# A convolution and a low-rank mixing block on one core: remainders of u read from PSUM, the first batch's last z added later in the chain, and a new order of the work

## The chip, the cores and the metric

The kernel runs on one core of a Trainium2 chip. The metric is the device time of one execution in microseconds (us). Five instruction queues matter: TensorE (PE, matmuls; its weight loads are shown apart as PEld), VectorE (DVE), ScalarE (ACT), GpSimd (POOL) and SyncE (SP), which here only issues DMAs. Each works through its own queue strictly in the order in which the program was written; an instruction that waits holds everything behind it on its engine. The on-chip memories are SBUF and PSUM; PSUM has eight banks of 2 KB per partition, and matmuls write only there.

## The reference

Eight batches of a sequence of 4224 positions and 192 features go through two stages. All arithmetic is float32; U, V and the two channel weights come in as float64.

```python
# stage 1: a causal convolution over 7 taps with softmax weights for each position and head
w = softmax(weight_gen, axis=-1)            # (8, 4224, 8 heads, 7 taps)
x_unf = x_pad[:, idx, :].reshape(B, S, K, H, group)      # group = 24 features a head
y = einsum('bshk,bskhg->bshg', w, x_unf).reshape(B, S, D)

# stage 2: mixing along the sequence (rank 32), then a channel MLP
u  = y + ((y^T @ U) @ V)^T                  # U: 4224 x 32, V: 32 x 4224
out = u + relu(u @ w_ch1) @ w_ch2           # 192 -> 768 -> 192
```

The mixing needs y of a whole batch (as z = U^T y) before u of any position of that batch is known.

## The kernel before

**Tiles and stages.** A batch is cut into 11 chunks of 3 x 128 positions, so there are 88 chunks (convolution) and 88 blocks (MLP), numbered through. Chunk or block i belongs to batch i // 11. The convolution runs about 11 chunks ahead of the MLP. A chunk is seven products x * w ("p"; POOL makes most of them two taps at a time, DVE some in the first batch), which are added in a PSUM accumulator "acc": in the first batch mostly on PE, by multiplying with an identity, later on DVE. The finished chunk is y in SBUF. It is split into a high and a low float32r part ("yhl", ACT and POOL), and three matmuls add its part of z ("zp").

**The end of a batch.** `z_sum`, `z_split` and `z_copy` (from line 634) add up the parts of z (ACT, then DVE), multiply by `rsum` on PE ("zr") and copy the result as high and low parts into `zcat` (ACT, DVE, ACT). In the first batch z is computed from y as it is, without the split (`z_first`), and with `zcat` there MLP block 0 can begin.

**u in two orders.** Each block needs u twice. With positions on the partitions it is the start value of the output ("ab"): `u_seed`, `u_mix` and `u_take` copy y to a PSUM bank, add V^T z on PE, and copy the sum into an SBUF tile `uts[i]`. With features on the partitions it is the input of the first MLP matmul: `u_turn` transposes u on DVE and sends it through DRAM, `u_back` fetches it as `uT` (two parts: 128 and 64 features), `u_hi` (ACT) rounds it to float32r ("hi") and `u_lo` (DVE) subtracts this from it ("lo", the remainder). For blocks 0, 1 and every block whose number divides by 11 ("late" blocks), whose z is not there in time, y itself is turned, and V^T z is added in PSUM (`d_seed`, `d_mix`); their hi and lo are then read from that PSUM bank "d". The pool `ps_d` holds one bank; "u" and "d" take turns in it.

**The MLP.** `mm1` makes one of six hidden parts h of a block with five matmuls: hi against the high and low weights, lo against the high ones, and both 64-feature parts. `g_hi` (ACT, relu) and `g_lo` (DVE) split h into gh and gl. `mm2` adds them into "ab", and `out_half` (ACT) and `out_add` (DVE) make the output "o". h has two banks, "ab" has two.

**What sets the order.** Until MLP block 0 the order of the work ("the fill") is the written list `FIRST`: each code stands for one step, and each step issues on one engine (S softmax, P and C the splitting of the float64 inputs, M a product, F and A an addition to acc, Y the copy to y, Z its part of z, x and W loads, and so on). After it a planner takes over: `lay_block` and `lay_conv` give every step a due time, from tables with one number for each kind of step (`GHI`, `ADD`, `UH`, ...), in units of a sixth of a block, and `issue` writes the steps in the order of these numbers. On PE, z's matmuls are slipped in between those of `mm2`.

All instructions are recorded through one helper, so the profile names line 30 for nearly all of them; they are told apart by the tiles that they write and read.

Of the kernel before, what the change touches and what calls it, by code (L numbers as in the profile page):

```python
# [44 lines left out]
def conv_moe_kernel(  # L45
# [23 lines left out]
    P = 128  # L69
# [6 lines left out]
    PAD = K - 1  # L76

# [8 lines left out]
    yp = ctx.enter_context(tc.tile_pool(name="yp", bufs=12))  # L86
# [9 lines left out]
    ps_a = ctx.enter_context(tc.tile_pool(name="ps_a", bufs=1, space=PS))  # L96

# [89 lines left out]
    def f64_split(name, raw, n, hi, shaped, lo=None, rest=None, after=None):  # L187
# [201 lines left out]

    works = {}  # L390
# [60 lines left out]
    def conv_wq(c):  # L451
        if not wq3:
            wq3.append(ps_first.tile([P, 512], F32, tag="wq", name="wq"))
        n, jl = where[c]
        nc.scalar.copy(wq_of(c), ws[n][:, jl : jl + T])
# [7 lines left out]
    p_count = {1: 0, 2: 0}  # L463

    def p_tile(c, n, shape, name):


        more = {1: 4, 2: 1}[n]
        turn = p_count[n] % (2 + more)
        p_count[n] += 1  # L470
        if c <= NB and turn > 1:
            return pf.tile(shape, F32, tag=f"p{n}", name=name, bufs=more)
        return pp.tile(shape, F32, tag=f"p{n}", name=name)

    def conv_mul(c, k, mixed=False):
        n, jl = where[c]
        j = c % NB * T
        pk = p_tile(c, 1, [P, T, D], f"p_{c}_{k}")
# [10 lines left out]
    def conv_mul2(c, k):  # L489
# [3 lines left out]
        pk = p_tile(c, 2, [P, 2, T, D], f"p_{c}_{k}{k + 1}")  # L493
# [120 lines left out]
    def z_first(c):  # L614
# [19 lines left out]
    def z_sum(b):  # L634
        assert b == 0 or z_made[0] == (b + 1) * NB
# [4 lines left out]
        if b == 0:  # L640
            nc.scalar.copy(zs, zp[:, :D])
        else:
            zt = zpool.tile([NU * R, D], F32, tag="zt", name=f"zt_{b}")
            nc.scalar.copy(zt, zp[:, D:])
            nc.vector.tensor_tensor(zs, zp[:, :D], zt, op=ALU.add)
# [26 lines left out]
    uts = {}  # L672
# [19 lines left out]
    def u_take(i, t0, nt):  # L692
        if t0 == 0:
            u_tile(i)
        if t0 + nt == T:
            ys.pop(i)
        nc.scalar.copy(
            uts[i][:, t0 : t0 + nt, :].rearrange("p t d -> p (t d)"),
            upre.pop((i, t0, "mixed")),
        )  # L700
        if t0 + nt == T:
            whole.add(i)

    def u_copy(i):
        u_tile(i)
        nc.scalar.copy(uts[i], ys.pop(i))

    def u_tile(i):
        uts[i] = up.tile([P, T, D], F32, tag="u", name=f"u_{i}", bufs=4)
        if is_late(i):  # L710
            whole.add(i)
# [41 lines left out]
    def d_tile(i, part, pool=None):  # L753
        d = (pool or ps_d).tile(
            [P, 512], F32, tag="px" if pool else "d", name=f"d_{i}_{part}",
# [3 lines left out]
    def d_turn(i, part):  # L759

        d_tile(i, part, ps_first if part else None)
# [25 lines left out]
    def u_from(i, part):  # L787
        if is_late(i):
# [3 lines left out]
    def like(i, ap):  # L792
        return ap if is_late(i) else rows(ap)
# [68 lines left out]
    def ab_seed(i, t):  # L862
        assert i in whole
# [81 lines left out]
    def is_late(i):  # L945
        return i % NB == 0 or i == 1
# [18 lines left out]
    def soften(n):  # L965
# [4 lines left out]
    GHI = [0.422, 0.497, 0.855, 0.085, 1.172, 0.203]  # L970
    GLO = [1.211, 0.996, 1.747, 1.065, 1.826, 0.888]
    AB = [-0.628, -0.6, -0.164]
    OH = [1.964, 2.844, 2.312]
    OA = [3.093, 3.481, 2.941]
    UC = 2.94
    UT = -7.829
    UB = -5.438
    UH = [-1.151, -0.59]
    UL = [-0.6, 0.072]
    DS = [-1.819, -0.718]  # L980
    US = [-11.639, -9.443]
# [12 lines left out]
    ZML = 1.655
    ZS = 2.991
    ZP = 3.105
    ZC = 4.259
    M1 = [0.262, -0.107, 0.14, -0.282, -0.017, -0.391]
    M2 = [-0.081, -0.032, 1.559, 0.826, 0.748, 0.146]
    DM = [-1.621, -0.684]  # L1000
    ZM = 4.798
# [194 lines left out]
```

## Time and profile before

| | |
|---|---|
| median of 3 runs | 1093.28 us (1092.83 to 1094.02) |
| the profiled execution, first to last instruction (span) | 1093.1 us |
| first MLP matmul ("h") starts | 90.12 us |
| PE busy | 1067.9 us (98%) |
| DVE busy | 935.5 us (86%) |
| POOL busy | 850.1 us (78%) |
| ACT busy | 793.8 us (73%) |
| granted TensorE clock, mean | 0.998 |

The span of the profiled execution and the median of the runs are 0.2 us apart. The profile's busy times count an engine's own instructions; a matmul's end is modelled, so that PE's busy share by itself does not tell how much of a stretch is waiting. The rows further down are therefore read with their starts and counts.

### The profile page before, as it was taken

How to read it: one execution, taken by the hardware profiler on the slowest of the kernel's cores; microseconds unless marked ns; L12 is line 12 of the kernel's file. 1: busy time of each engine (PE TensorE's matmuls, PEld its weight loads, DVE VectorE, ACT ScalarE, POOL GpSimd, SP SyncE). 2: the span in 40 equal slices, each digit the busy share in tenths (PEclk: the TensorE clock that was granted, in tenths of full speed). 3: DMA queues.
4: the chain of work that ended last, by engine and by line, in shares of the span. 5: the costliest groups of instructions: out<-in, count | busy, mean ns of one | idle time of the engine just before them, and what ended most of it. 6: DMA issues, size and time to landing. Idle time of an engine off the chain costs nothing.

```text
span 1093.1 us, 20252 instructions
## 1 busy us (share of the span) xinstructions
PE 1067.9 (98%) x6634; PEld 1041.6 (95%) x6634; DVE 935.5 (86%) x1714; ACT 793.8 (73%) x1894; POOL 850.1 (78%) x467
## 2 busy tenths in 40 slices
PE   5988989999999999999999999999999999999998
PEld 4767989999999999999999999999999999999998
DVE  6987999998999998998999988998999988855553
ACT  4676667777777777787777777687777777676664
POOL 6996999898998989989998989989998989500000
PEclk9999999999999999999999999999999999999999
DMA  7861534444434534345343544435444333333331
GB/s 208 247 196 37 138 111 125 118 137 122 137 111 120 159 101 142 114 115 152 105 144 108 145 122 118 141 97 151 117 127 125 107 98 91 91 91 84 99 91 51
DMA packets 132619, 133.67 MB, mean 122 GB/s; under 512 B 80681, under 2 KB 106537, under 8 KB 132386
## 3 DMA queue, kind: packets, MB, share of 16 engines
q1 hardware_dynamic: 132514, 132.38, 42.7%
q8 instruction: 52, 0.85, 0.3%
q14 instruction: 53, 0.43, 0.1%
HBM read 79.10 MB, written 53.23 MB: 121 GB/s over the span
## 4 chain that ended last, share of the span: by engine, by line
PE 86%; DVE 5%; DMA 3%; ACT 2%; issue 2%; POOL 1%; SPq 1%; DVEq 0%; ACTq 0%; POOLq 0%
PE h L30 40%; PE ab L30 39%; PE zp L30 3%; PE u L30 2%; DVE acc L30 2%; DMA x<-in_x_dram 1%; POOL p L30 1%; DVE lo L30 1%; PE acc L30 1%; DMA vq<-vt 1%; DVE gl L30 1%; SPq L30 1%; DMA vt<-v_hi 0%; DVE p L30 0%; DVE sm L30 0%
## 5 line engine op out<-in xcount | busy, mean ns | idle before, releaser
L30 POOL TENSOR_TENSOR p<-x,wr 128x1152 f32<-128x1152 f32 (+1 forms) x333 | 665.2, 2018 | 80.0 <-DVE acc L30 70.3
L30 PE MATMUL ab<-w2c,gh 128*128 128x384 f32 x1584 | 482.5, 354 | 0.7 <-ACT ab L30 0.7
L30 ACT ACTIVATE gh<-h 128x384 fp32r<-128x384 f32 x528 | 258.4, 492 | 164.6 <-PE h L30 158.1
L30 PE MATMUL ab<-w2c,gl 128*128 128x192 f32 x1584 | 371.7, 254 | 0.0
L30 DVE SCALAR_TENSOR_TENSOR gl<-h,gh 128x384 fp32r<-128x384 f32 x528 | 281.6, 550 | 77.0 <-ACT gh L30 74.8
L30 DVE TENSOR_TENSOR acc<-acc,p 128x576 f32<-128x576 f32 x402 | 301.2, 749 | 2.5 <-ACT acc L30 2.1
L30 PEld LDWEIGHTS ab<-w2c,gl 128*128 128x128 f32 x1584 | 297.8, 190 | 0.0
L30 PEld LDWEIGHTS ab<-w2c,gh 128*128 128x128 f32 x1584 | 292.2, 188 | 1.4 <-ACT ab L30 1.4
L30 PE MATMUL h<-hi,w1h 128*128 128x384 f32 x528 | 182.3, 345 | 0.5 <-DVE gl L30 0.5
L30 PE MATMUL h<-lo,w1s 128*128 128x384 f32 x528 | 179.4, 340 | 2.0 <-DVE lo L30 1.8
L30 PE MATMUL h<-lo,w1h 128*128 128x384 f32 x528 | 178.4, 338 | 0.0
L30 PE MATMUL h<-hi,w1s 128*128 128x384 f32 x528 | 178.2, 338 | 0.0
L30 PE MATMUL h<-hi,w1l 128*128 128x384 f32 x528 | 178.1, 337 | 0.0
L30 ACT COPY o<-ab 128x192 f32<-128x192 f32 x264 | 84.6, 320 | 72.8 <-PE ab L30 63.0
L30 ACT ACTIVATE ab<-u 128x384 f32<-128x384 f32 x264 | 130.0, 492 | 7.1 <-DVE o L30 6.3
L30 POOL TENSOR_TENSOR yhl<-y,yhl 128x576 fp32r<-128x576 f32 x77 | 128.0, 1663 | 5.1 <-ACT yhl L30 5.1
L30 DVE TENSOR_TENSOR lo<-uT,hi 128x384 fp32r<-128x384 f32 (+1 forms) x158 | 116.1, 735 | 13.2 <-ACT hi L30 13.1
L30 PEld LDWEIGHTS h<-lo,w1s 128*128 128x128 f32 x528 | 99.4, 188 | 4.7 <-DVE lo L30 4.6
L30 PEld LDWEIGHTS h<-hi,w1h 128*128 128x128 f32 x528 | 100.1, 190 | 3.6 <-DVE gl L30 3.0
L30 PEld LDWEIGHTS h<-hi,w1l 128*128 128x128 f32 x528 | 99.7, 189 | 0.0
L30 PEld LDWEIGHTS h<-lo,w1h 128*128 128x128 f32 x528 | 99.4, 188 | 0.0
L30 PEld LDWEIGHTS h<-hi,w1s 128*128 128x128 f32 x528 | 99.4, 188 | 0.0
(123 smaller groups left out, 1184.4 us busy)
## 6 DMA issues: line engine op xcount, KB each, us to landing
turn<-sq SPq DMA_DIRECT2D x348, 72.0 KB, 1.9
out_dram<-o SPq DMA_DIRECT2D x87, 288.0 KB, 2.7
x<-in_x_dram SPq DMA_DIRECT2D x77, 288.0 KB, 3.0
uT<-turn SPq DMA_DIRECT2D x87, 192.0 KB, 2.7
uT<-turn SPq DMA_DIRECT2D x174, 96.0 KB, 2.7
wr<-in_weight_gen_dram SPq DMA_DIRECT2D x15, 336.0 KB, 3.2
x<-in_x_dram SPq DMA_DIRECT2D x7, 504.0 KB, 5.6
wr<-in_weight_gen_dram SPq DMA_DIRECT2D x9, 252.0 KB, 2.8
```

Source lines behind the costliest of these rows:

```text
L30: return self.tc.keep_in_program_order(call(*args, **kwargs))
```

## The change

Five things change.

1. **hi and lo from PSUM in more blocks.** A new test `by_psum(i)` is true for blocks 2 to 10 (the rest of the first batch) and for the last two blocks of every later batch (20, 21, 31, 32, ...). For these, `d_seed` copies uT into the PSUM bank "d" (ACT), and `u_hi` and `u_lo` read that bank. The set of late blocks is the same as before, written as a tuple.
2. **u goes back into y.** `u_take` writes into the y tile instead of a tile of its own; the copy `u_copy` of the late blocks is gone, and the y pool has 16 buffers instead of 12.
3. **PSUM pools of the first batch.** The pool of h ("ps_h", two banks) is opened at the start, and the first batch's scratch banks ("x", "wq", the second "d") come from it rather than from a pool that is closed before the MLP begins.
4. **z of chunk 10.** In the first batch, z of chunks 0 to 9 is summed and multiplied by `rsum` (`z_rest`); chunk 10's part is then added to the result by three matmuls with `u4`, the sum of the three parts of U, repeated four times (`make_u4`, `z_last`).
5. **A new order.** The list is written in another order (which product takes a buffer of the first batch's own pool is now said in the list, N instead of M), and nearly all numbers of the planner's tables change.

```diff
-    yp = ctx.enter_context(tc.tile_pool(name="yp", bufs=12))
+    yp = ctx.enter_context(tc.tile_pool(name="yp", bufs=YU))
...
+    ps_h = ctx.enter_context(tc.tile_pool(name="ps_h", bufs=2, space=PS))
...
-                pool, tag = (ps_d, "d") if what == "t" else (ps_first, "px")
+                pool, tag = (ps_d, "d") if what == "t" else (ps_h, "h")
...
+    def make_u4():
+        u4 = yhp.tile([P, T, 2 * D], F32, tag="yhl", name="u4")
+        u4 = u4[:, :, : 4 * R].rearrange("p t (n r) -> p t n r", n=4)
+        part = [ucat[:, NJ - T :, n * R : (n + 1) * R].bitcast(F32) for n in range(NU)]
+        nc.vector.tensor_tensor(u4[:, :, 0], part[0], part[1], op=ALU.add)
+        nc.vector.tensor_tensor(u4[:, :, 0], u4[:, :, 0], part[2], op=ALU.add)
+        nc.scalar.copy(u4[:, :, 1:], u4[:, :, :1].to_broadcast([P, T, 3, R]))
+        u4s.append(u4)
+
+    def z_rest():
+        zs = zs2[0][: NU * R]
+        nc.scalar.copy(zs, zps[0][: NU * R, :D])
+        zr = zps[0][:, D : 2 * D]
+        nc.tensor.matmul(zr, rsum, zs2[0], start=True, stop=False, skip_group_check=True)
+        zrs[0] = zr
+
+    def z_last():
+        for t in range(T):
+            nc.tensor.matmul(
+                zrs[0], u4s[0][:, t].rearrange("p n r -> p (n r)"), ys[NB - 1][:, t, :],
+                start=False, stop=(t == T - 1), skip_group_check=True,
             )
...
         nc.scalar.copy(
-            uts[i][:, t0 : t0 + nt, :].rearrange("p t d -> p (t d)"),
+            ys[i][:, t0 : t0 + nt, :].rearrange("p t d -> p (t d)"),
             upre.pop((i, t0, "mixed")),
         )
...
     def d_seed(i, part):
         d_tile(i, part)
         nc.scalar.copy(rows(dpre[(i, part)]), turned(uTs[i][part]))
+        if not is_late(i):
+            dsum[(i, part)] = dpre.pop((i, part))
...
     def u_from(i, part):
-        if is_late(i):
+        if is_late(i) or by_psum(i):
             return dsum[(i, part)]
         return turned(uTs[i][part])
...
     def is_late(i):
-        return i % NB == 0 or i == 1
+        return i in LATE
+
+    def by_psum(i):
+        return not is_late(i) and (i < NB or i % NB in BACK)
...
-    GHI = [0.422, 0.497, 0.855, 0.085, 1.172, 0.203]
+    LATE = (0, 1, 11, 22, 33, 44, 55, 66, 77)
+    BACK = (9, 10)
+    DS2 = [-2.413, -0.59]
+    GHI = [0.877, 0.218, 0.821, -0.124, 1.106, 0.271]
...
-        M11.3v A10.4t M11.5v M11.4p A10.6t P10.3 P10.4 A11.0v Y10 P10.5 Z8 Z9 P10.1 A11.1v
-        P10.6 A11.4v A11.5v P10.7 M11.6p Z10 P10.8 A11.3v d0 d1 D11 Y11.6
+        Y10 z1 P10.8 z2 C9.1 N11.4p A11.4v d1 d0 D11 A11.5v A11.3v z3 Y11.6 m0 h0 m1 l0
+        h1 l1 D8
...
         for part in range(2):
-            at(t0 + UH[part], u_hi, i, part)
-            at(t0 + UL[part], u_lo, i, part)
+            uh, ul = (UH2, UL2) if by_psum(i) else (UH, UL)
+            at(t0 + uh[part], u_hi, i, part)
+            at(t0 + ul[part], u_lo, i, part)
+            if by_psum(i):
+                at(t0 + DS2[part], d_seed, i, part)
```

Three places show how the queues move. The first is PE's queue early in the fill, while chunk 0 is added up; "acc" is the accumulator of a chunk, "p_01" a product of taps 0 and 1, "pt_v_t" the bank in which a piece of V is being split. Before:

```order
L30 MATMUL acc_189<-p_01_174,ident 128x288 x2
L30 MATMUL pt_v_t<-v_hi,sign_130 128x330
L30 MATMUL acc_189<-p_5_205,ident 128x288 x2
L30 MATMUL acc_189<-p_6_208,ident 128x288 x2
L30 MATMUL acc_254<-p_0_239,ident 128x288 x2
L30 MATMUL acc_254<-p_3_229,ident 128x288 x2
L30 MATMUL pt_u_t<-ucat,sign_130 128x384
```

And now:

```order
L30 MATMUL pt_v_t<-v_hi,sign_136 128x330
L30 MATMUL acc_190<-p_01_181,ident 128x288 x2
L30 MATMUL acc_190<-p_5_200,ident 128x288 x2
L30 MATMUL acc_190<-p_6_231,ident 128x288 x2
L30 MATMUL acc_259<-p_0_224,ident 128x288 x2
L30 MATMUL pt_u_t<-ucat,sign_136 128x384
L30 MATMUL acc_259<-p_3_267,ident 128x288 x2
```

The piece of V moves ahead of the second half of p_01, and the piece of U ahead of p_3 of chunk 1; the additions keep their number.

The second is PE's queue at the end of the fill, from the last chunk's z to the first MLP matmuls of block 0 ("d" is u of block 0 with features on the partitions, "ab_-1" two start-up matmuls without use for the result). Before:

```order
L30 MATMUL zp_350<-y_776,ucat 96x192 x2
L30 MATMUL d_0_802<-ident,y_265 128x128 [waits Activation_49]
L30 MATMUL d_0_802<-ident,y_265 128x128 x2
L30 MATMUL d_1_806<-ident,y_265 64x128 x3
L30 MATMUL zr_814<-zs_109,rsum 128x192 [waits Activation_49]
L30 MATMUL d_0_802<-vcat,zcat_111 128x384 [waits DVE_49]
L30 MATMUL d_1_806<-vcat,zcat_111 64x384
L30 MATMUL ab_-1_0_841<-vcat 128x384 [waits DVE_49,PE_49]
L30 MATMUL ab_-1_1_843<-vcat 128x384
L30 MATMUL h_0_847<-hi_0_820,w1h 128x384
```

And now:

```order
L30 MATMUL zp_356<-zs_112,rsum 128x192 [waits Activation_49]
L30 MATMUL zp_356<-y_796,u_618 128x192 x3
L30 MATMUL d_1_808<-ident,y_280 64x128 x3
L30 MATMUL d_0_812<-ident,y_280 128x128 [waits Activation_49]
L30 MATMUL d_0_812<-ident,y_280 128x128 x2
L30 MATMUL d_0_812<-vcat,zcat_114 128x384 [waits DVE_49]
L30 MATMUL d_1_808<-vcat,zcat_114 64x384
L30 MATMUL ab_-1_0_844<-vcat 128x384 [waits PE_49]
L30 MATMUL ab_-1_1_846<-vcat 128x384
L30 MATMUL h_0_856<-hi_0_825,w1h 128x384 [waits Activation_49]
L30 MATMUL h_0_856<-hi_0_825,w1l 128x384
L30 MATMUL h_0_856<-lo_0_828,w1h 128x384 [waits DVE_49]
```

The product with `rsum` now stands before the last chunk's three matmuls, and the two start-up matmuls and the first of h no longer wait for DVE; the third of h does.

The third is ACT's queue at the end of block 20 and the start of block 21 ("hi_21" belongs to block 21, "u_0" to a block of the next batch that shares the bank with "d", "zt" to the batch's z). Before:

```order
L30 ACTIVATE gh_4_4296<-h_4_4250 128x384 [waits PE_49]
L30 ACTIVATE gh_5_4298<-h_5_4272 128x384 [waits PE_49]
L30 ACTIVATE ab_0_4300<-u_3880 128x384 [waits DVE_49,Activation_49]
L30 CAST hi_21_4304<-uT_21_4175 128x384 [waits DMAHW7_49,DMAHW6_49]
L30 COPY zt_4314<-zp_2700 96x192 [waits PE_49]
L30 COPY o_4153<-ab_2_4248 128x192 [waits PE_49]
L30 COPY u_0_4336<-y_2731 128x384
L30 ACTIVATE gh_0_4338<-h_0_4327 128x384 [waits PE_49]
```

And now:

```order
L30 ACTIVATE gh_4_4308<-h_4_4277 128x384 [waits PE_49]
L30 ACTIVATE gh_5_4311<-h_5_4283 128x384 [waits PE_49]
L30 ACTIVATE ab_0_4313<-y_2259 128x384 [waits DVE_49]
L30 COPY d_1_4315<-uT_21_4202 128x384 [waits DMAHW7_49,DMAHW6_49]
L30 CAST hi_21_4317<-d_1_4315 128x384 [waits Activation_49]
L30 COPY o_4174<-ab_2_4258 128x192 [waits PE_49]
L30 COPY u_0_4344<-y_2765 128x384 [waits DVE_49]
L30 COPY zt_4354<-zp_2753 96x192
L30 ACTIVATE gh_0_4357<-h_0_4346 128x384 [waits PE_49]
```

The copy of uT into "d" stands ahead of hi, "u_0" has a wait for DVE (which reads "d" for lo), and "zt" has moved behind "o" and "u_0", still ahead of gh_0.

## Rows read from the trace of the kernel before

**Rows 1.** The page's first part: busy time, share of the span and number of instructions of each engine.

```profile
PE 1067.9 (98%) x6634; PEld 1041.6 (95%) x6634; DVE 935.5 (86%) x1714; ACT 793.8 (73%) x1894; POOL 850.1 (78%) x467
```

**Rows 2.** Busy time of the engines in six stretches (start:end, length, then for PE, PEld, DVE, ACT and POOL the busy us and the number of instructions, the granted clock, the DMA share and GB/s): the fill from PE's first additions to the last chunk's z, and then stretches of 20 us, three of the first batch, one of steady work, one across the end of a batch.

```profile
12.96:87.16 74.20, 70.02 (x296) 54.02 (x296) 66.53 (x112) 48.57 (x93) 68.49 (x39) 1.00 0.69 206
...
120.00:140.00 20.00, 19.14 (x123) 18.68 (x122) 18.16 (x31) 13.21 (x33) 16.84 (x10) 1.00 0.43 119
140.00:160.00 20.00, 18.94 (x121) 18.23 (x119) 18.71 (x35) 14.42 (x37) 19.91 (x11) 1.00 0.41 111
160.00:180.00 20.00, 19.02 (x119) 18.32 (x120) 18.74 (x32) 14.17 (x35) 18.92 (x12) 1.00 0.42 127
260.00:280.00 20.00, 20.00 (x130) 20.00 (x129) 17.93 (x34) 14.82 (x37) 17.57 (x10) 1.00 0.46 129
320.00:340.00 20.00, 19.98 (x125) 19.16 (x124) 18.76 (x34) 13.29 (x33) 17.57 (x11) 1.00 0.44 132
```

**Rows 3.** The timeline of PE early and at the end of the fill (start, us, engine, operation, tile written <- tiles read, count, and the idle time before with what ended it).

```profile
12.96 7.83 PE L30 MATMUL acc<-p,ident 128*128 128x288 f32 x20 [3.68 <-DVE p L30]
20.41 0.53 PE L30 MATMUL pt_v_t<-v_hi,sign 128*128 128x330 f32 x1
20.78 4.04 PE L30 MATMUL acc<-p,ident 128*128 128x288 f32 x16
...
51.01 2.11 PE L30 MATMUL zp<-y,ucat 128*96 128x192 f32 x12
...
87.16 0.62 PE L30 MATMUL d<-vcat,zcat 128*128 128x384 f32 x2 [1.00 <-DVE zcat L30]
89.70 0.41 PE L30 MATMUL ab_-1_0_841<-vcat 128*128 128x384 f32 x1 [1.92 <-DVE lo L30]
...
90.12 0.45 PE L30 MATMUL h<-hi,w1h 128*128 128x384 f32 x1
...
91.66 0.52 PE L30 MATMUL h<-hi,w1h 128*128 128x384 f32 x1
```

**Rows 4.** The list of waits of the stretch from 12 to 87 us, for the engine and tile that waited and what it waited for: total us, times, longest.

```profile
ACT v_r L30 <- PE pt_v_t L30: 4.9, 2, 4.3
...
DVE pt_u_t L30 <- ACT pt_u_t L30: 2.0, 1, 2.0
...
DVE acc L30 <- ACT acc L30: 1.3, 1, 1.3
DVE w_s L30 <- ACT w2c L30: 1.3, 1, 1.3
```

**Rows 5.** The timeline of DVE at the end of the fill.

```profile
85.95 0.76 DVE L30 TENSOR_TENSOR y<-acc,p 128x576 f32<-128x576 f32 x1
86.74 0.36 DVE L30 TENSOR_TENSOR zcat<-zr,zcat 32x192 fp32r<-32x192 f32 x1
88.15 0.56 DVE L30 TENSOR_TENSOR lo<-d,hi 128x384 fp32r<-128x384 f32 x1 [1.05 <-ACT hi L30]
89.00 0.55 DVE L30 TENSOR_TENSOR lo<-d,hi 64x384 fp32r<-64x384 f32 x1 [0.29 <-ACT hi L30]
```

**Rows 6.** The timeline of ACT at the same place.

```profile
87.64 1.33 ACT L30 CAST hi<-d 128x384 fp32r<-128x384 f32 x3 [0.26 <-PE d L30]
```

**Rows 7.** The view of tile lo, which groups all instructions that write it or read it (count, duration in ns as min/median/max, first and last start in us, forms): uT is in SBUF, d in PSUM, hi in SBUF.

```profile
L30 DVE TENSOR_TENSOR lo<-uT,hi x158: 536/710/2344, 109.9 to 1073.7; 128x384 fp32r<-128x384 f32 x79, 64x384 fp32r<-64x384 f32 x79
L30 DVE TENSOR_TENSOR lo<-d,hi x18: 536/552/558, 88.2 to 967.2; 128x384 fp32r<-128x384 f32 x9, 64x384 fp32r<-64x384 f32 x9
```

**Rows 8.** The timeline of DVE: single lo instructions in the first batch and in blocks 20 and 21.

```profile
135.50 1.94 DVE L30 TENSOR_TENSOR lo<-uT,hi 64x384 fp32r<-64x384 f32 x1
...
160.36 2.34 DVE L30 TENSOR_TENSOR lo<-uT,hi 64x384 fp32r<-64x384 f32 x1
...
328.26 1.50 DVE L30 TENSOR_TENSOR lo<-uT,hi 128x384 fp32r<-128x384 f32 x1 [0.36 <-ACT hi L30]
...
331.81 1.61 DVE L30 TENSOR_TENSOR lo<-uT,hi 64x384 fp32r<-64x384 f32 x1
```

**Rows 9.** The timeline of POOL beside them.

```profile
327.91 1.43 POOL L30 TENSOR_TENSOR yhl<-y,yhl 128x576 fp32r<-128x576 f32 x1
329.31 3.70 POOL L30 TENSOR_TENSOR p<-x,wr 128x576 f32<-128x576 f32 x2
```

**Rows 10.** The list of waits of the stretch from 120 to 170 us.

```profile
PE h L30 <- DVE lo L30: 1.8, 2, 1.0
...
PEld ab L30 <- ACT ab L30: 1.0, 1, 1.0
```

**Rows 11.** The list of waits of the weight loads alone, from 200 to 960 us.

```profile
PEld h L30 <- DVE lo L30: 2.1, 6, 0.4
PEld h L30 <- DVE gl L30: 2.1, 7, 0.3
```

**Rows 12.** Groups of ACT's instructions by line and tile with forms kept apart (busy us, mean ns | idle before).

```profile
L30 ACT CAST hi<-d 128x384 fp32r<-128x384 f32 x17 | 8.2, 481 | 5.7 <-PE d L30 5.6
L30 ACT COPY d<-uT 128x384 f32<-128x384 f32 x16 | 7.8, 489 | 0.3
```

**Rows 13.** The timeline of ACT in block 22, a late block: the copy of y for a later u, and the gh behind it.

```profile
344.73 0.48 ACT L30 COPY u<-y 128x384 f32<-128x384 f32 x1 [0.39 <-DVE lo L30]
345.38 0.49 ACT L30 ACTIVATE gh<-h 128x384 fp32r<-128x384 f32 x1 [0.17 <-PE h L30]
```

More of the change, by code (lines that the diff above doesn't have):

```diff
@@ L452, in conv_wq @@
         if not wq3:
[L453 removed]
+            wq3.append(ps_h.tile([P, 512], F32, tag="h", name="wq"))
         n, jl = where[c]
@@ L461, in wq_of, with p_tile, conv_mul @@
         )
[L463 to L472, printed above, removed]
+    def p_tile(n, shape, name, own=False):
+        if own:
+            return pf.tile(shape, F32, tag=f"p{n}", name=name, bufs={1: 4, 2: 1}[n])
         return pp.tile(shape, F32, tag=f"p{n}", name=name)
-    def conv_mul(c, k, mixed=False):
+    def conv_mul(c, k, mixed=False, own=False):
         n, jl = where[c]
         j = c % NB * T
-        pk = p_tile(c, 1, [P, T, D], f"p_{c}_{k}")
+        pk = p_tile(1, [P, T, D], f"p_{c}_{k}", own)
         eng, w = (nc.vector, wq_of(c)) if mixed else (nc.gpsimd, ws[n][:, jl : jl + T])
@@ L639, in z_sum @@
         zs = zs2[b % 2][: NU * R]
[L640 to L645, printed above, removed]
+        zt = zpool.tile([NU * R, D], F32, tag="zt", name=f"zt_{b}")
+        nc.scalar.copy(zt, zp[:, D:])
+        nc.vector.tensor_tensor(zs, zp[:, :D], zt, op=ALU.add)
         zsums[b] = zs
@@ L754, in d_tile @@
         d = (pool or ps_d).tile(
-            [P, 512], F32, tag="px" if pool else "d", name=f"d_{i}_{part}",
+            [P, 512], F32, tag="h" if pool else "d", name=f"d_{i}_{part}",
         )
@@ L759, in d_turn @@
     def d_turn(i, part):
-        d_tile(i, part, ps_first if part else None)
+        d_tile(i, part, ps_h if part else None)
         d = dpre[(i, part)]
@@ L792, in like @@
     def like(i, ap):
-        return ap if is_late(i) else rows(ap)
+        return ap if is_late(i) or by_psum(i) else rows(ap)
     def u_hi(i, part):
@@ new lines, in conv_moe_kernel @@
+    ADD = [0.508, 1.464, 2.749, 3.76, 4.58, 5.857]
+    LA = 0.044
+    STEPS = [5.931, 5.923, 5.438, 6.078, 5.586, 5.067, 5.209, 5.963, 6.029, 5.979]
+    SOFT = [-8.354, -8.975, -3.589, -2.399, -7.352, -5.008, -1.783]
+    DN = 5.961
+    YH = 1.477
+    YHL = 0.698
+    YLL = 0.701
+    YL = 3.359
+    ZML = 2.117
+    ZS = 3.629
+    ZP = 3.685
+    ZC = 3.799
+    M1 = [0.6, -0.031, -0.492, -1.208, 0.023, -0.777]
+    M2 = [0.482, 0.155, 0.849, 0.04, 0.636, 0.709]
+    DM = [-1.792, -0.153]
@@ L1057, in conv_moe_kernel @@
                 conv_wq(*n)
-            elif kind == "M":
-                conv_mul2(*n) if by == "d" else conv_mul(*n, by == "v")
+            elif kind in "MN":
+                own = kind == "N"
+                conv_mul2(*n, own) if by == "d" else conv_mul(*n, by == "v", own)
             elif kind == "D":
@@ L1083, in conv_moe_kernel @@
                 d_turn(0, *n)
-        z_sum(0)
-        z_split(0)
-        z_copy(0)
-        for part in range(2):
-            d_mix(0, part)
-            u_hi(0, part)
-            u_lo(0, part)
+            elif kind == "z":
+                (make_u4, z_rest, z_last, lambda: z_copy(0), warm_up)[n[0]]()
+            elif kind == "m":
+                d_mix(0, *n)
+            elif kind == "h":
+                u_hi(0, *n)
+            elif kind == "l":
+                u_lo(0, *n)
     gp = ctx.enter_context(tc.tile_pool(name="gp", bufs=2 * NM))
-    ps_h = ctx.enter_context(tc.tile_pool(name="ps_h", bufs=2, space=PS))
     ps_ab = ctx.enter_context(tc.tile_pool(name="ps_ab", bufs=2, space=PS))
```

127 lines of the change are left out of this document (52 added, 75 removed).

## The prediction

> **What bounds the kernel now.** I read the page's busy times first. PE is busy 98% of the span, DVE 86%, POOL 78%, ACT 73% [rows 1]; the reader sees one engine that is nearly full, but not where its other 2% lie. For that I cut the span into stretches and counted PE's matmuls, since a matmul's modelled end hides short waits but a count doesn't. Steady work does 130 matmuls in 20 us, with PE busy all of them; the first batch does 123, 121 and 119, and the stretch with the end of a batch 125 [rows 2]. So steady blocks are bound by PE's own work, of which the change takes nothing, and PE loses time in three places only: the fill, the first batch, and the end of each batch.
>
> In the fill, from 12.96 to 87.16 us, PE is busy 70.0 us of 74.2, POOL 68.5 and DVE 66.5 [rows 2]. Nobody waits much, and three engines share the bound. At the end of the fill the chain is serial: zcat on DVE at 86.74 [rows 5], d on PE at 87.16 [rows 3], hi on ACT from 87.64 [rows 6], lo on DVE from 88.15 and 89.00 [rows 5], and only then, 89.70, PE's start-up matmuls, with h at 90.12 [rows 3].
>
> In the first batch I looked for what ends PE's waits, and found DVE's lo, 1.8 us in 50, and ACT's ab, 1.0 [rows 10]. The view of tile lo says why lo is late: read from uT in SBUF it takes 536 ns at best, 710 in the median and 2344 at worst; read from d in PSUM it takes 536 to 558, all 18 of them [rows 7]. The long ones stand beside POOL. At 328.26 a lo takes 1.50 us, and ends at 329.76, where POOL's yhl ran until 329.34; one from 331.81 ends at 333.42, where POOL's two products end at 333.01 [rows 8, 9]. Each ends some 0.4 us behind an end on POOL, as if it began only then.
>
> **The change part by part.** The sum is made against the profiled execution's span, 1093.1 us; the median of the runs is 0.2 above it.
>
> *The fill's order.* The additions on PE stay the same in number (their row: 16 in 4.04 us). In the old order a piece of V is transformed behind chunk 0's first additions, and ACT waits 4.3 us for it; DVE waits 2.0 for ACT's piece of U [rows 3, 4]. Both pieces now stand earlier on PE. But a wait that goes shortens the fill only as far as the three full engines let it: PE has 74.2 - 70.0 = 4.2 us to give, POOL 5.7, DVE 7.7 [rows 2]. The new order also adds to DVE two small additions for u4, which no row shows; the nearest is zcat's, 32x192 in 0.36 us [rows 5], so between 0.2 and 0.75 for the pair. The products with u4 replace three of the same width, and the copies of u4 are ACT's, which is busy 48.6 of the 74.2. Bounds: -4.2, if PE's idle time went entirely, and +3, if the list lays a new wait nearly as long as the longest, 4.3, on an engine that is full; DVE's 1.3 us waits for ACT [rows 4] are of the kind that can appear anywhere else. I take -2.5, a little over half of PE's idle time.
>
> *The end of the fill.* h_0 now waits for hi alone, and the start-up matmuls for nothing on DVE; only the third matmul of h waits for lo. Before, from zcat's start to the second h: 91.66 - 86.74 = 4.92 us [rows 3, 5]. Now d at +0.42, hi at +0.90, its end at +1.4, two matmuls of h until about +2.0, and the rest after the second lo, +2.85 by [rows 5] (89.55 - 86.74 = 2.81); the second h follows at about +3.2. That is 1.7 less. Also y of the next chunk, 0.76 on DVE ahead of zcat [rows 5], moves behind it, which is counted in the term above. Bounds: -1.0 (lo is as late and PE waits at the third matmul) and -2.4 (lo also earlier). Value: -1.7.
>
> *lo from PSUM in blocks 2 to 10.* The three stretches lack 7, 9 and 11 matmuls against 130, so (7+9+11)/130 x 20 = 4.2 us in all [rows 2]. The change can reach the part that hangs on lo. A wait of PE for it is 1.8 directly [rows 10]; ACT's ab, next in the list, waits for others, and DVE, freed of stretched lo's of 1.94 and 2.34 us where 0.55 would do [rows 8], gets to everything behind them sooner. Bounds 0 and -4.2; value -2.7, about two thirds.
>
> The Trainium skill ("VectorE: DVE Perf Modes", the section on the TRN2 errata) speaks against this part: it charges VectorE 120 fixed cycles from PSUM and 58 from SBUF, and by its clock of 0.96 GHz that makes 65 ns more, or about 3 us of DVE over 46 instructions. The trace disagrees for this form: 552 ns in the median from d, 536 at best from uT [rows 7]; by the page's figure, were all 3 us to reach PE, the sum would be -6.7.
>
> *The same at seven ends of a batch.* The stretch from 320 to 340 lacks 5 matmuls, 5/130 x 20 = 0.77 us [rows 2]. From 200 to 960 us the weight loads wait 2.1 us for lo and 2.1 for gl, which comes behind lo on DVE [rows 11]. Bounds 0 and 7 x 0.77 = -5.4. Half of it is what I take: -2.8, 0.4 at each end, since gl, ab and z's copies have their own lateness there.
>
> *What it costs ACT.* Of 23 blocks two parts each get a copy into d: 46 x 0.489 = 22.5 us on ACT; hi then takes 0.481 [rows 12]. Nine u_copies fall away, left uncounted. ACT idles 1093.1 - 793.8 = 299 us [rows 1], and this idle time covers the copies: I take nothing. If it isn't where they stand, they make gh late; that is the last rival. The bank pools and the other planner numbers change when things are issued, not how many: nothing, with PE's order in a steady block unchanged.
>
> Sum: -2.5 - 1.7 - 2.7 - 2.8 = -9.7, span 1083.4, with the 0.2 above it **1083.6 us**. Two thirds of the sum is -6.5, four thirds -12.9: 1080.4 to 1086.8, its own range.
>
> **The rivals.**
> - *The fill keeps its length* (its term is 0). For it: three engines have only 4 to 8 us idle in 74, so that a wait removed comes back elsewhere. Against: the waits removed are the longest there [rows 4]. 1093.3 - 7.2 = 1086.1.
> - *The relief of lo doesn't reach PE.* The two lo terms give 0.5 each. For it: PE waits directly for lo only 1.8 us in the first batch. Against: DVE is full 18.2 to 18.7 of 20 us there [rows 2, 10]. 1093.3 - 4.2 - 1.0 = 1088.1.
> - *Nothing nets.* The fill gets longer by the u4 work and a new wait, 2 to 3 us, that eats up the 1.7 at its end and what lo gives: about 1093.
> - *The one bank "d" becomes the wait* (slower). In 23 blocks the pool of one bank now holds two tiles of d, whose last reader is DVE, between those of u. The copy "u_0" stands on ACT ahead of gh_0 and waits for lo; gh_0 then comes late, and PE, with two banks of h, stands still. Where d had this bank before, ACT did wait: 0.39 us at 344.73, but the gh behind it waited another 0.17 for PE, so nothing was lost [rows 13]. If there were no such slack, a lo of 0.552 [rows 7] a block makes 23 x 0.552 = 12.7, and the two lo terms, from the same blocks, don't come: 1093.3 - 4.2 + 12.7 = 1101.8. It decides the sign from 4.2/23 = 0.18 us of PE time a block.
>
> The Trainium skill ("PSUM — Partial Sum Buffer", the section on bank collisions) has two engines never in one bank at a time, so the seed's wait could not be dropped; the wait at 344.73 agrees, though it shows a program's order and no collision.
>
> **How the numbers follow.** My forecast 0.48, the kept fill 0.16, no relief 0.12, nothing nets 0.10, the bank 0.14. What this kernel's measurement can tell from no change is about 0.2%, 2.2 us. The first three are faster: 0.76; nothing nets is the same: 0.10; the bank is slower: 0.14. The range goes from 1078, close to where all four terms are at their lower bounds (-16.2), to 1093.5, which takes in "nothing nets" and leaves the bank out. Left out are 0.14 and some 0.04 below.
>
> **What would show it.** The fill: first h at 85 to 87 instead of 90.12, and the second h about 3.2 behind zcat. Blocks 2 to 10: lo<-d at 0.55 and no lo above 1 us there, and 127 to 130 matmuls per 20 us. Ends of batches: 128 to 130, and the weight loads' waits for lo and gl smaller than 2.1 each. Wrong if the fill's end doesn't move, if matmul counts stay at 119 to 123 though all lo's take 0.55, or if ACT's copy of y into u waits for lo in most of the 23 blocks and the gh behind it no longer waits for PE.

## The result and the profile after

The changed kernel takes 1102.2 us (median of 4 runs, 1102.11 to 1103.53) against 1093.65 of the kernel before beside it: ratio 1.0078, interval 1.0064 to 1.0093. It is slower by 8.6 us, where 1083.6 was forecast.

The page's busy line of the changed kernel, which answers to [rows 1]:

```profile
PE 1066.5 (97%) x6634; PEld 1037.6 (94%) x6634; DVE 972.2 (88%) x1716; ACT 809.8 (74%) x1932; POOL 837.7 (76%) x467
```

DVE is busy 37 us longer, with two instructions more; POOL is 12 us shorter. The 20 us stretches of [rows 2] in the changed kernel (columns as there):

```profile
120.00:140.00 20.00, 20.00 (x130) 20.00 (x129) 17.76 (x34) 16.50 (x40) 17.07 (x10) 1.00 0.51 147
140.00:160.00 20.00, 20.00 (x129) 19.98 (x129) 19.02 (x35) 17.05 (x41) 19.92 (x13) 1.00 0.45 129
160.00:180.00 20.00, 20.00 (x130) 20.00 (x130) 18.63 (x35) 16.99 (x42) 18.84 (x12) 1.00 0.49 141
260.00:280.00 20.00, 19.40 (x125) 19.03 (x124) 19.72 (x35) 14.65 (x36) 17.73 (x10) 1.00 0.36 97
320.00:340.00 20.00, 20.00 (x130) 19.88 (x129) 17.24 (x34) 16.04 (x41) 16.59 (x10) 1.00 0.43 127
```

The first batch has gained what was to be had: 130, 129 and 130 matmuls instead of 123, 121 and 119, and the end of a batch 130 instead of 125. The loss stands where the kernel before had none: 260 to 280 falls from 130 to 125. Put together from the starts of the blocks' first h in both traces (us):

| | before | after | difference |
|---|---|---|---|
| first h of block 0 | 90.12 | 85.47 | -4.65 |
| blocks 0 to 10 | 129.47 | 123.43 | -6.04 |
| blocks 11 to 76 | 747.74 | 765.84 | +18.10 |
| block 77 to the end | 125.73 | 125.63 | -0.10 |
| span | 1093.1 | 1100.4 | +7.3 |

In blocks 11 to 76 four blocks of each batch, the 1st, 4th, 5th and 8th (11, 14, 15, 18, then 22, 25, 26, 29, ...), rise from 11.2 or 11.3 to between 12.05 and 12.17; the others change by less than 0.45. Six batches times four make 24 blocks. The list of waits from 240 to 960 us, which holds 23 of them (total, times, longest):

```profile
ACT ab L30 <- DVE o L30: 28.2, 23, 1.2
PEld ab L30 <- ACT ab L30: 19.6, 23, 0.9
...
PE ab L30 <- ACT ab L30: 13.7, 23, 0.6
...
ACT u L30 <- DVE lo L30: 2.0, 5, 0.4
```

PE waits for ab, which waits for o on DVE; u waits for lo hardly ever. And tile lo, for [rows 7]:

```profile
L30 DVE TENSOR_TENSOR lo<-uT,hi x112: 515/626/2602, 216.6 to 1059.8; 128x384 fp32r<-128x384 f32 x56, 64x384 fp32r<-64x384 f32 x56
L30 DVE TENSOR_TENSOR lo<-d,hi x64: 517/550/559, 85.4 to 1081.4; 128x384 fp32r<-128x384 f32 x32, 64x384 fp32r<-64x384 f32 x32
```

From d it never takes over 0.559 us. From uT it now takes up to 2.602. Block 14 shows the chain, with lo of the block after it. DVE:

```profile
249.88 0.78 DVE L30 STREAM_TRANSPOSE sq<-y 128x576 f32<-128x576 f32 x1
250.58 0.73 DVE L30 TENSOR_TENSOR acc<-acc,p 128x576 f32<-128x576 f32 x1
251.43 2.60 DVE L30 TENSOR_TENSOR lo<-uT,hi 128x384 fp32r<-128x384 f32 x1
253.95 0.35 DVE L30 TENSOR_TENSOR o<-ab,o 128x192 f32<-128x192 f32 x1
```

POOL, three products in one row and then yhl:

```profile
247.91 5.71 POOL L30 TENSOR_TENSOR p<-x,wr 128x1152 f32<-128x1152 f32 x3 [0.79 <-DVE acc L30]
253.58 1.72 POOL L30 TENSOR_TENSOR yhl<-y,yhl 128x576 fp32r<-128x576 f32 x1
```

ACT (yhl, hi, and the ab that comes late):

```profile
250.31 0.68 ACT L30 CAST yhl<-y 128x576 fp32r<-128x576 f32 x1
250.89 0.51 ACT L30 CAST hi<-uT 128x384 fp32r<-128x384 f32 x1
...
254.33 0.49 ACT L30 ACTIVATE ab<-y 128x384 f32<-128x384 f32 x1 [1.23 <-DVE o L30]
```

PE:

```profile
254.88 0.44 PE L30 MATMUL ab<-w2c,gh 128*128 128x384 f32 x1 [0.60 <-ACT ab L30]
```

hi ends at 251.40, and lo starts at 251.43. The addition before it on DVE ended at 251.31 and released POOL's third product, which ends at 253.62; single products of this size take 2.2, so it began at about 251.4, some hundredths ahead of lo. lo then ends 0.41 behind it, and o, ab and PE's next matmul are late in turn. Now the same block of the kernel before, on DVE:

```profile
260.07 0.78 DVE L30 STREAM_TRANSPOSE sq<-u 128x576 f32<-128x576 f32 x1 [0.65 <-ACT u L30]
260.78 0.74 DVE L30 TENSOR_TENSOR acc<-acc,p 128x576 f32<-128x576 f32 x1
261.42 0.54 DVE L30 TENSOR_TENSOR lo<-uT,hi 128x384 fp32r<-128x384 f32 x1
```

on POOL:

```profile
261.66 2.40 POOL L30 TENSOR_TENSOR p<-x,wr 128x1152 f32<-128x1152 f32 x1 [0.60 <-DVE acc L30]
```

and on ACT:

```profile
260.85 0.52 ACT L30 CAST hi<-uT 128x384 fp32r<-128x384 f32 x1
```

There DVE's transpose sq waits 0.65 for ACT's copy of u, so the addition ends at 261.52, after hi (261.37). lo follows it without a gap, at 261.42 (the records of successive DVE instructions overlap by up to 0.1), and POOL's third product starts only at 261.66; it is POOL that takes longer, 2.40 instead of 2.2, which costs nobody anything. In the new order the wait of sq is gone, the addition comes 0.44 earlier in the block (6.79 instead of 7.23 behind the block's first h), hi only 0.2. The removed wait had decided which of the two engines goes first.

### The profile page after: what moved, and what is told of

It reads as the page before. It is cut to its first block, busy times and chain, and to the rows that moved or that the text cites. A ratio compares the mean times of both kernels' runs of the same rounds, so it can differ in the third digit from the quotient of the medians.

```text
span 1100.4 us, 20192 instructions
## 1 busy us (share of the span) xinstructions
PE 1066.5 (97%) x6634; PEld 1037.6 (94%) x6634; DVE 972.2 (88%) x1716; ACT 809.8 (74%) x1932; POOL 837.7 (76%) x467
## 4 chain that ended last, share of the span: by engine, by line
PE 81%; ACT 6%; DVE 5%; issue 4%; DVEq 0%; ACTq 0%
PE h L30 38%; PE ab L30 36%; PE zp L30 3%; PE u L30 2%; DVE lo L30 2%; ACT yhl L30 1%; ACT acc L30 1%; PE acc L30 1%; ACT ab L30 1%; ACT hi L30 1%; ACT y L30 1%; DVE o L30 1%; DVE acc L30 1%; DVE p L30 1%; PE d L30 0%
## 5 line engine op out<-in xcount | busy, mean ns | idle before, releaser
L30 POOL TENSOR_TENSOR p<-x,wr 128x1152 f32<-128x1152 f32 x333 | 655.4, 1987 | 72.6 <-DVE acc L30 64.6
L30 PE MATMUL ab<-w2c,gh 128*128 128x384 f32 x1584 | 497.0, 354 | 14.3 <-ACT ab L30 14.3
L30 PE MATMUL ab<-w2c,gl 128*128 128x192 f32 x1584 | 364.2, 256 | 0.0
L30 ACT ACTIVATE ab<-y 128x384 f32<-128x384 f32 x264 | 129.8, 492 | 32.0 <-DVE o L30 31.1
L30 POOL TENSOR_TENSOR yhl<-y,yhl 128x576 fp32r<-128x576 f32 x77 | 124.9, 1622 | 8.3 <-DVE sq L30 6.2
L30 DVE TENSOR_TENSOR lo<-uT,hi 128x384 fp32r<-128x384 f32 x112 | 116.1, 1036 | 6.4 <-ACT hi L30 2.0
L30 DVE TENSOR_TENSOR o<-ab,o 128x192 f32<-128x192 f32 x264 | 91.4, 346 | 10.9 <-ACT o L30 8.9
```

The lines of the kernel that those rows point to most:

```text
L30: return self.tc.keep_in_program_order(call(*args, **kwargs))
```

## The experiments

The theory that the runs were to test is called the lost start: lo with two operands in SBUF waits for a running POOL instruction, and the new order lets POOL start first in these blocks. The rival is the one on record, the bank d and ACT's copies. The expectations count 28 such blocks, four for seven batches; it is 24, since the last batch has no convolution beside it and the first reads lo from PSUM. With 0.87 each that is 20.9 us, not 24.4.

**hi one place earlier.**

```diff
-    UH = [-1.266, -0.087]
+    UH = [-1.45, -0.087]
```

> The changed kernel with one number of the planner's table changed: hi of the first part moves one place up in ACT's queue, ahead of yhl, in the steady blocks. Theory (the lost start): in 28 blocks lo of the next block waits some 0.1 us for hi, POOL's third product starts in that gap, and lo stretches from 0.54 to 2.60 us; with hi earlier lo starts behind acc and ahead of POOL, no lo lasts over 1 us, POOL's product takes about 2.4 instead of 2.2, and the 28 blocks of 12.06 to 12.17 us go back to 11.2 or 11.3: 1102.2 - 28 x 0.87 = 1077.8, between 1076 and 1080. Rival (the bank and ACT's copies): copies into the one PSUM bank d make ACT late; they all stay, so the time stays at 1101 to 1103.

Measured: 1087.9 us (1087.44 to 1088.47), 0.9947 of the kernel before, interval 0.9933 to 0.9961. It is 14.3 us faster than the changed kernel with every copy in place, but 10 above the expectation. The longest lo is now another. DVE in block 14 and at its end:

```profile
251.09 0.54 DVE L30 TENSOR_TENSOR lo<-uT,hi 128x384 fp32r<-128x384 f32 x1
...
253.82 1.70 DVE L30 TENSOR_TENSOR lo<-uT,hi 64x384 fp32r<-64x384 f32 x1
```

POOL there:

```profile
253.68 1.43 POOL L30 TENSOR_TENSOR yhl<-y,yhl 128x576 fp32r<-128x576 f32 x1
```

The first lo has its start back and takes 0.54. But the second lo now comes 0.14 behind the start of POOL's yhl and takes 1.70. Part of the loss moved on to another lo; the theory holds for the place and missed this. The rival, which forecast 1101 to 1103, is refuted.

**Four more blocks of a batch from PSUM.**

```diff
-    BACK = (9, 10)
+    BACK = (1, 4, 5, 8, 9, 10)
```

> The changed kernel with four more blocks of every later batch (1, 4, 5 and 8 counted in the batch) whose hi and lo read the PSUM bank d; the queues are the same but for the copies. These are the 28 blocks whose lo lasts 2.60 us. The lost start: a lo that reads only one operand from SBUF does not wait for POOL, so lo takes 0.55 though it starts at the same place, and the time is 1077.8, between 1076 and 1081. Rival (the bank and ACT's copies): 28 more blocks with two copies each and lo's in the bank's turn make it slower still, by up to 28 x 0.55 = 15: 1102 to 1117, with ACT waiting for lo at u in them.

Measured: 1084.48 us, 0.9914 (0.9899 to 0.9929): 17.7 us faster than the changed kernel, with 56 copies more on ACT. Its tile lo:

```profile
L30 DVE TENSOR_TENSOR lo<-d,hi x120: 519/549/558, 85.8 to 1063.9; 128x384 fp32r<-128x384 f32 x60, 64x384 fp32r<-64x384 f32 x60
L30 DVE TENSOR_TENSOR lo<-uT,hi x56: 515/551/2608, 228.5 to 1031.6; 128x384 fp32r<-128x384 f32 x28, 64x384 fp32r<-64x384 f32 x28
```

No lo from d is long. One lo of 2.60 a batch is left among those from uT, in a block that had none in the changed kernel (the 7th of a batch, 12.08 us long). ACT's u did wait for lo, 18.2 us in all, and PE lost nothing by it in the other blocks.

**The kernel before with the wait taken away.** One number of the old table.

```diff
-    UTK = [-9.526, -7.934]
+    UTK = [-9.526, -8.3]
```

> The kernel before with one number changed: ACT's second copy of u out of its bank moves ahead of the copy into acc, so that DVE's transpose no longer waits 0.65 us for it (25.4 us of waiting in 240 to 960 us go). Nothing of PSUM is changed. The lost start: DVE's next addition to acc ends 0.5 to 0.65 us earlier, releases POOL's third product before lo can start, and lo lasts over 2 us in the blocks without a softmax reduction, four or more of every batch: at least 28 x 0.85 = 24 us slower, 1115 to 1125. Rival (the bank and ACT's copies): a wait of 25 us less on DVE and no copy added: the same or faster, 1085 to 1094.

Measured: 1117.04 us, 1.0214 (1.0196 to 1.0233). In block 14, DVE:

```profile
258.05 0.77 DVE L30 STREAM_TRANSPOSE sq<-u 128x576 f32<-128x576 f32 x1
258.74 0.73 DVE L30 TENSOR_TENSOR acc<-acc,p 128x576 f32<-128x576 f32 x1
260.11 2.26 DVE L30 TENSOR_TENSOR lo<-uT,hi 128x384 fp32r<-128x384 f32 x1 [0.63 <-ACT hi L30]
```

and POOL:

```profile
256.38 5.57 POOL L30 TENSOR_TENSOR p<-x,wr 128x1152 f32<-128x1152 f32 x3 [0.27 <-DVE acc L30]
```

sq has no wait, the addition comes early, POOL's third product runs until 261.95, and lo ends 0.42 behind that. One due time, by which DVE loses these waits (25.4 us of them from 240 to 960), costs 23 us in the old kernel, with nothing of PSUM changed. The rival forecast the other sign.

**The PSUM blocks alone, in the kernel before.**

```diff
+        if not is_late(i):
+            dsum[(i, part)] = dpre.pop((i, part))
...
-        if is_late(i):
+        if is_late(i) or by_psum(i):
...
+    BACK = (9, 10)
+    DS2 = [-1.85, -0.59]
+    UH2 = [-1.45, -0.575]
+    UL2 = [-1.032, 0.072]
```

> The kernel before with the PSUM bank for hi and lo alone: blocks 2 to 10 and the last two blocks of every later batch, with due times for the copies that fit the old table (four numbers; all others stay). The lost start: the steady blocks keep their 11.2 us; blocks 2 to 10 gain some 5 us and each end of a batch 0.8, so 1093.5 - 5.3 - 7 x 0.8 = 1082.6, between 1081 and 1087. Rival (the bank and ACT's copies): 23 blocks in which gh_0 is late by up to 0.55: 1094 to 1106.

Measured: 1087.56 us, 0.9944 (0.9925 to 0.9963; the single runs spread from 1084.2 to 1090.1). The part that the change is named for makes the kernel faster by itself, by 6.6 us. That is less than expected: the time lies 0.6 above the range given. In its trace blocks 2 to 10 take 103.13 and the last two blocks of a batch 23.1, where the changed kernel has 101.40 and 22.8, so the expectation, which took its gains from there, counted gains of the new table too. Its lo's from uT stay under 0.9 us.

**All blocks, and seven of each later batch, from PSUM.**

```diff
-    BACK = (9, 10)
+    BACK = (1, 2, 3, 4, 5, 6, 7, 8, 9, 10)
```

> The changed kernel with hi and lo from the PSUM bank d in every block but block 0 and the late ones, which have it already, so that no lo reads uT any more. The lost start: the one lo of 2.60 us in every later batch that was left in the run more_psum (the block eighth in its batch) takes 0.55 too, and no other can appear: 1084.5 - 6 x 0.88 = 1079.2, between 1078 and 1081.5. Rival (the bank and ACT's copies, now as a limit that comes with more blocks): u's copy waited 18.2 us for lo in 29 places of more_psum and will wait in some 50; if PE's slack is used up there, blocks rise over 11.3 and the time is 1084 to 1095.

Measured: 1079.69 us, 0.9875 (0.9858 to 0.9891). Its tile lo and its waits of u, from 240 to 960 us:

```profile
L30 DVE TENSOR_TENSOR lo<-d,hi x176: 517/550/560, 85.9 to 1058.7; 128x384 fp32r<-128x384 f32 x88, 64x384 fp32r<-64x384 f32 x88
```

```profile
ACT u L30 <- DVE lo L30: 24.8, 52, 0.9
```

u waits for lo in 52 places, 24.8 us in all, and the steady blocks take 11.18: the bank's wait that the rival priced is there, and PE loses nothing by it. With `BACK = (1, 4, 5, 7, 8, 9, 10)`:

> As more_psum, and the eighth block of every later batch too, so that only the blocks with a softmax reduction between acc and lo still read uT. The lost start: lo of those blocks starts with acc as before and stays under 1 us, so the time is that of all_psum within 1 us: 1079.2, between 1078 and 1082. Rival (the stretch moves on): each cure has let the next block's lo lose its start, as more_psum did; then one or more blocks of 12.07 us a batch remain and the time is 1084 to 1086.

Measured: 1079.54 us, 0.9871 (0.9856 to 0.9885), no lo over 0.66. The two can't be told apart; nothing moved on this time.

**The old numbers in the changed kernel.** `GHI` to `ZM` of the kernel before, the due times of the PSUM blocks' copies, hi and lo (`DS2`, `UH2`, `UL2`) as in before_psum_only, everything else as in the changed kernel.

> The changed kernel with the planner's numbers of the kernel before (all but the due times of the copies into d, which are those of before_psum_only): the new list of the fill, z of chunk 10 added later and the PSUM blocks stay. The lost start, with the numbers as the only cause of the loss: before_psum_only (1087.6) with a fill that is 4.6 us shorter: 1083.0, between 1081 and 1085, no lo over 1 us after block 10. Rival (the pools, the y buffers or the later z take part in the loss): blocks of 12 us appear in later batches with the old numbers too: 1090 or more.

Measured: 1084.14 us, 0.9913 (0.9898 to 0.9928); no lo over 0.74 in it. With the new list, the pools, the y buffers and the later z in place there is no loss; it comes with the table.

**No PSUM blocks.**

```diff
-        return not is_late(i) and (i < NB or i % NB in BACK)
+        return False
```

> The changed kernel without the PSUM blocks: hi and lo read uT in all but the late blocks, all other parts of the change stay. The lost start: the 28 long lo's stay and others come in blocks 2 to 10 and at the ends of batches, 0.85 us each for 10 to 25 of them: 1110 to 1123. Rival (the bank and ACT's copies): 46 copies less on ACT: 1085 to 1100.

Measured: 1116.55 us, 1.021 (1.0194 to 1.0225): 14.4 us slower without the 46 copies. Its tile lo, where 158 are again from uT as in the kernel before:

```profile
L30 DVE TENSOR_TENSOR lo<-uT,hi x158: 515/710/2601, 103.2 to 1095.0; 128x384 fp32r<-128x384 f32 x79, 64x384 fp32r<-64x384 f32 x79
```

**The wait put back into the changed kernel.**

```diff
-    DS2 = [-2.413, -0.59]
+    DS2 = [-2.2, -0.59]
...
-    UTK = [-10.239, -8.549]
+    UTK = [-10.239, -8.25]
```

> The changed kernel with a wait put back: ACT's second copy of u out of its bank moves behind the copy into acc (and the copies into d of the PSUM blocks by as much, to keep the bank's turns), so that DVE's transpose waits for it again, some 0.45 to 0.65 us a block. hi stays where it is in ACT's queue. The lost start: acc then ends after hi, lo starts right behind acc and ahead of POOL's product, and the 28 lo's of 2.60 us are gone: 1102.2 - 24.4 = 1077.8, between 1076 and 1083. Rival (a wait more on DVE costs what it lasts): 40 waits of 0.5 on an engine that is 88% busy: 1102 to 1115.

Measured: 1078.79 us, 0.9862 (0.9844 to 0.988): 23.4 us faster than the changed kernel, and within a microsecond of the three runs with most blocks from PSUM. Block 14 on DVE, on POOL, and then tile lo and the waits of sq from 240 to 960 us:

```profile
248.46 0.78 DVE L30 STREAM_TRANSPOSE sq<-y 128x576 f32<-128x576 f32 x1 [0.55 <-ACT y L30]
249.16 0.73 DVE L30 TENSOR_TENSOR acc<-acc,p 128x576 f32<-128x576 f32 x1
249.81 0.54 DVE L30 TENSOR_TENSOR lo<-uT,hi 128x384 fp32r<-128x384 f32 x1
```

```profile
250.04 2.40 POOL L30 TENSOR_TENSOR p<-x,wr 128x1152 f32<-128x1152 f32 x1 [0.57 <-DVE acc L30]
```

```profile
L30 DVE TENSOR_TENSOR lo<-uT,hi x112: 518/546/724, 215.9 to 1035.9; 128x384 fp32r<-128x384 f32 x56, 64x384 fp32r<-64x384 f32 x56
```

```profile
DVE sq L30 <- ACT y L30: 21.9, 42, 0.6
```

sq waits 0.55, lo is ahead of POOL again by 0.23, no lo takes over 0.724, and with 42 waits put back on DVE, 21.9 us in this stretch, the kernel is more than 20 us faster. PE's order in block 14, which differs in a few places from the kernel before, is that of the changed kernel here too, so it wasn't PE's order that cost the time.

**The old z of chunk 10, in all_psum.**

```diff
-        ... Y10 z1 P10.8 z2 C9.1 ...
+        ... Y10 Z10 P10.8 z1 C9.1 ...
```

(and `z0` left out, the chunk's part in `z_first` again)

> all_psum without the later z of chunk 10: all 11 chunks are summed in the old way, the copy of the sum and the product with rsum stand behind the last y again, and u4 is not made. If the old chain set the start of zcat, the copy (0.32) and the product (0.4) now come back into it: 1079.7 + 0.8 = 1080.5. If DVE's additions ahead of zcat set it (ACT's half of zcat was done 0.7 us before DVE began its own in all_psum), nothing moves: 1079.2 to 1080.0, and first h at 85.9 as there.

Measured: 1079.08 us, 0.9863 (0.9843 to 0.9884). The end of the fill on PE:

```profile
82.75 0.59 PE L30 MATMUL zp<-zs,rsum 128*128 128x192 f32 x2 [0.40 <-ACT zs L30]
...
84.51 0.62 PE L30 MATMUL d<-vcat,zcat 128*128 128x384 f32 x2 [0.52 <-DVE zcat L30]
...
85.53 0.44 PE L30 MATMUL h<-hi,w1h 128*128 128x384 f32 x1
```

The product with rsum comes 0.9 us later than in all_psum (81.86 there), zcat doesn't, and the first h is at 85.53 against 85.91. The fourth part of the change buys nothing that these runs can tell.

## Why the prediction was wrong

**The step that failed** is the last sentence on costs: "The bank pools and the other planner numbers change when things are issued, not how many: nothing, with PE's order in a steady block unchanged." It put the numbers' effect at nothing. The new table as a whole makes the kernel 18.1 us slower (1102.2 against 1084.14 in old_numbers), and two of its due times alone are worth 23.1: blocks 11 to 76 take 765.84 in the changed kernel and 742.74 in late_take, which differs from it in these two. The rows for it were in the forecast: it had read that a lo with uT ends 0.4 us behind POOL, and used this only for the blocks where such lo's go away. It didn't ask of the blocks that still read uT whether POOL or DVE would now start first. No rival asked it either; the one that forecast a loss looked for it in ACT's queue.

**The rival that came close in time was wrong too.** It gave 1101.8, measured is 1102.2, by another way: u waits for lo no more than before (2.0 us from 240 to 960, as the list of waits shows; the kernel before has 2.0 there too), and the two lo terms, which it struck out, came in full. A time that agrees doesn't show a mechanism.

**The fill.** Forecast -2.5 for the order; zcat starts at 84.04 instead of 86.74, -2.70. DVE and PE of the changed kernel:

```profile
84.04 0.36 DVE L30 TENSOR_TENSOR zcat<-zp,zcat 32x192 fp32r<-32x192 f32 x1
```

```profile
85.47 0.44 PE L30 MATMUL h<-hi,w1h 128*128 128x384 f32 x1
...
87.19 0.34 PE L30 MATMUL h<-hi,w1h 128*128 128x384 f32 x1
```

Not all of that is the order. POOL's first product waits for the first transfer of x, and this landed at another time in each execution. POOL in the kernel before, in the changed kernel, and in before_early_take, which has the old list:

```profile
12.09 2.22 POOL L30 TENSOR_TENSOR p<-x,wr 128x1152 f32<-128x1152 f32 x1 [3.61 <-DMA x<-in_x_dram]
```

```profile
11.01 2.22 POOL L30 TENSOR_TENSOR p<-x,wr 128x1152 f32<-128x1152 f32 x1 [1.51 <-DMA x<-in_x_dram]
```

```profile
8.94 2.22 POOL L30 TENSOR_TENSOR p<-x,wr 128x1152 f32<-128x1152 f32 x1 [0.86 <-DMA x<-in_x_dram]
```

From this product to zcat it is 74.65 us before and 73.03 now. So the order gives 1.62, and 1.08 is x, which came earlier. The three traces with the old list take 74.65 to 75.45 here, the nine with the new one 73.03 to 73.80, on the mean 1.6 less. Whether the new list also brings x earlier isn't shown: the product starts at 8.94, 11.50 and 12.09 with the old list and at 10.12 to 11.10 with the new.

Forecast -1.7 for the fill's end; from zcat to the second h it was 3.15 instead of 4.92, -1.77. Here the clock has a part that the forecast didn't see. In the kernel before, PE had waited 1.00 us for zcat and 1.92 for lo [rows 3], and then its granted clock was at the lower level, 0.50 (1.2 GHz; columns as in [rows 2]):

```profile
90.20:93.60 3.40, 3.40 (x13) 3.40 (x12) 1.13 (x2) 1.14 (x3) 0.00 (x0) 0.50 0.00 0
```

The first two h lie 1.54 apart there [rows 3]. In before_early_take, with the same list and the same two waits, the clock stayed at 1.00. DVE and PE:

```profile
84.39 0.36 DVE L30 TENSOR_TENSOR zcat<-zr,zcat 32x192 fp32r<-32x192 f32 x1
```

```profile
87.78 0.33 PE L30 MATMUL h<-hi,w1h 128*128 128x384 f32 x1
...
88.66 0.34 PE L30 MATMUL h<-hi,w1h 128*128 128x384 f32 x1
```

The first two h are 0.88 apart, and from zcat to the second it is 4.27. So the shorter chain is worth 1.12 at the full clock, and 0.65 is the clock. It fell at this place in two of the three traces with the old list and in none of the nine with the new one. Both sizes came out, then, but partly by luck: of 4.47 us, 2.74 are the two mechanisms that were forecast. The credit to the later z is not borne out, and how the rest divides over the list's many moves wasn't tried.

**lo from PSUM.** Blocks 2 to 10 went from 106.75 to 101.40, -5.35 where -2.7 was forecast with -4.2 as its bound: the bound counted only 60 of their 107 us. The ends of batches gave about 0.8 each at five ends and 0.35 at the last; with 0.4 for seven ends the forecast had half the size and one end too many. With the old table, in before_psum_only, blocks 2 to 10 gain 3.6 and an end 0.43, close to what was forecast; the rest comes from the two together, since with the new table alone, in no_psum, blocks 2 to 10 take 109.28. That a lo from d isn't held up by POOL is seen at 333.65, beside POOL's work:

```profile
333.65 0.56 DVE L30 TENSOR_TENSOR lo<-d,hi 128x384 fp32r<-128x384 f32 x1 [0.62 <-ACT hi L30]
```

```profile
329.85 5.58 POOL L30 TENSOR_TENSOR p<-x,wr 128x1152 f32<-128x1152 f32 x3 [1.00 <-DVE acc L30]
```

It runs beside a POOL product and takes 0.56. It is so in all twelve traces: 626 lo's from d start with at least 0.05 us of a POOL instruction left to run, and none takes over 0.56. Of the lo's from uT, 669 start so, and every one ends 0.41 to 0.51 behind that instruction's end; 440 start with POOL idle and take 0.515 to 0.562.

By the Trainium skill ("SBUF — State Buffer", the section "SBUF: two separate sides") a VectorE instruction with two SBUF inputs and a GpSimd instruction that reads SBUF exclude each other, and the one that starts second is blocked until the first ends. All the lo's here agree: 2.60 behind a POOL product, 0.55 with one operand in PSUM, and 2.40 instead of 2.2 for POOL when it is second.

**The base.** The profiled runs of this study lie 1.7 to 2.2 us above their spans (1102.15 and 1100.4 for the changed kernel). So the 0.2 between span and median in the forecast was too small by 1.5: the profiled execution of before was a long one of its kind, and runs of it spread from 1090.6 to 1096.6. Two reasons stand above. The transfer of x landed late in it: the first h came at 90.12, at 87.78 in before_early_take. And the clock fell in it: among the runs of before, the six with a mean granted clock of 0.996 or 0.997 took 1094.3 to 1096.6, the three with 1.000 took 1091.2 to 1093.1. What makes x land at such different times stays open.

## What to carry to other kernels

Where two engines can shut each other out, an edit of the order has to be checked in every block for who starts first, not only where it takes the conflict away: a few hundredths of a microsecond on an engine that isn't the bound cost 0.87 us of PE a block. A wait may hold such an order in place; before taking it away, look at what its engine releases sooner. An operand in PSUM took lo out of the conflict in every trace here, wherever it started, which is a safer cure than due times (hi_first moved part of the loss on to another lo). And where a kernel's executions spread by several microseconds, compare the stages of more than one trace before a gain is put down to the edit.

## What the hardware showed that was not expected

Who starts second pays very differently: POOL's product 0.18 us (2.40 for 2.22), DVE's lo 2.06 (2.60 for 0.54), since each waits for what is left of the other's work. In all traces POOL's 382 products of this size that start while a lo from uT runs take 2.23 to 2.58 us, and the 1974 others after 200 us take 2.21 to 2.25. And putting 21.9 us of waits (from 240 to 960 us) back on an engine that is busy 88% of the span made the kernel 23.4 us faster.
